# A quarter of the output projection in pieces of four matmuls between the last key tiles of attention

## The chip, the core and the metric

The kernel is one program on one core of a Trainium2 chip. The core has five engines that work side by side: TensorE (matrix products, PE in the profile, with its weight loads in a row PEld of their own), VectorE (DVE), ScalarE (ACT), GpSimd (POOL) and SyncE (SP, which here only issues DMAs). Products are accumulated in PSUM, which has eight banks of 128 x 512 numbers. The metric is the device time of one execution in microseconds; a run shown is one timed execution.

## The reference

Two blocks are applied twice to x, 2048 rows of 640 numbers, with the same weights: attention with 32 heads of 20, and a two-layer network with a squared relu. All is float32.

```python
        qkv = x @ wqkv                     # cut into q, k, v of 32 heads
        scores = jnp.einsum("bhqd,bhkd->bhqk", q, k) * (Dh ** -0.5)
        p = _softmax(scores, axis=-1)
        o = jnp.einsum("bhqk,bhkd->bhqd", p, v)
        return o.transpose(0, 2, 1, 3).reshape(B, S, D) @ wo
    x = x + _A_ref(_layernorm(x, axis=-1), A_wqkv, A_wo)
    x = x + _B_ref(_layernorm(x, axis=-1), B_w1, B_b1, B_w2, B_b2)
    # and both lines once more
```

The last product of `_A_ref`, with `wo`, is the output projection. It needs, for one row of x, the results of all 32 heads for that row.

## The kernel before

A layer is `qkv` (normalisation, projections to q, k and v, and some of the row maxima), `attention`, the output projection (`add_heads`), and `mlp`. Numbers that need full precision are kept as a high and a low half, and a product is three matmuls, high by high, high by low, low by high (`THREE`).

**Attention** works in 32 blocks (`NBLK`): 8 groups of four heads, and for each group four blocks of 512 queries (`NQB`, `QB`). A block has 16 key tiles of 128 keys (`NKT`). For one key tile TensorE forms four score tiles of 128 keys x 512 queries, one for each head (`score`, L755 of the profile). Each score matmul uses half the rows of the array, so that two run at once in two row tiles. ScalarE takes the exponential from PSUM to SBUF (`exps`, L765), and TensorE multiplies the four results with the values (`pv`, L770), eight matmuls of 32 columns each, in four column tiles. The values of all key tiles of a block gather in bank 7. Row maxima of later blocks come in between, a matmul (`smax`, L661) and a reduction on VectorE (L672).

**The order** on TensorE is a string. `ORDER_OF_BLOCK` names one letter per step: a and b are scores of one head, S is the scores of two heads with one exponential of 1024 columns, m and n are row maxima, V the values. The loop at the end of `attention` goes through the string and looks only at its end whether any row maximum is left; where none is, it goes on with `LAST_ORDER`, which has only S and V. `Clock` is a small model of the engines' times. It doesn't move any step of the string; it only says which bank a step gets, the one that it thinks free first. `clock.both` picks two neighbouring banks of 0 to 6 for an S.

**DMAs** go out on SP's queue in the order in which the program writes them; `begin` writes those that belong to a key tile as its first score is written (the dictionary `loads`, keyed by block and key tile). When a block is done, `finish` copies the sum out of bank 7, and `split` spreads the rest over the key tiles 4 to 12 of the next block: the denominators to HBM and back, their inverse on GpSimd (L814), the division (L825), the store of the block's result `ot` to `d_o`. For the very last block, inverse and division run on TensorE, VectorE and ScalarE, as `steps` that the projection takes up between its halves (`side`).

**The output projection** of a quarter of the rows (`qb`) loads five tiles `ot` of 128 of the 640 inner rows (`heads`), of which the fifth is complete only when the last group of heads is. `add_heads` then takes four tiles of 128 rows, each in two halves of 320 columns: 15 matmuls into one bank (`chain`, L336), an addition of x on VectorE (L1254), and after the second half a store to `x_mid`. Banks come from `ps_all`, a ring of all eight. After a quarter `layer` loads four slices of the weight `w_1`. Before the fourth quarter it starts `normal_rows`, which loads the first quarter's results again and normalises them for `mlp`.

Of the kernel before, what the change touches and what calls it, by code (L numbers as in the profile page):

```python
# [16 lines left out]
P = 128  # L17
# [5 lines left out]
KD = D // P  # L23
# [16 lines left out]
def tile_layers(  # L40
# [284 lines left out]
    def row_tile(src, r):  # L325
        t = xtile("x")
        dma(nc.sync, t, src[r * P : (r + 1) * P, :])
        return t
# [205 lines left out]
    class Clock:  # L534


        def __init__(self):
            self.free = [0] * 7
            self.lane, self.over, self.fresh, self.place = [0, 0], [0, 0], [False, False], 9
            self.now, self.load, self.values, self.since = 0, 0, False, 0  # L540
            self.act, self.act_end, self.dve = 0, 0, 0
            self.ready, self.used, self.acc = {}, [], 0
# [35 lines left out]
            return banks[:, b, :]  # L578

        def both(self, kt):  # L580
            b = min(range(6), key=lambda b: max(self.free[b : b + 2]))
            t = max(self.row(par, b + par) for par in range(2))
            if kt >= 3 and len(self.used) > kt - 3:
                t = max(t, self.used[kt - 3])
            t = max(t, self.act, self.act_end - 1958)
            self.act, self.act_end = t + 897, max(t + 1015, self.act_end + 910)
            self.free[b] = self.free[b + 1] = self.act_end
            self.ready[kt] = self.act_end + 80
            return banks[:, b : b + 2, :]
# [504 lines left out]
        "abmbmVbambannVbmabanmVSmbanVSnabmVSnSmVm"  # L1094
    )

    LAST_ORDER = "SSSVSSVSSVSV"

    def attention(first, x_src, first_rows):
        last = NBLK * NKT  # L1100
        es_of = {}
        e_n.clear()
        weights.extend(slot([P, 2, QB], F32, "e") for _ in range(6))
        st_n, sm_n = [0, 0], [0, 0]
        state = {"begun": -1, "done": 0, "acc": None, "debt": 0}
        clock = Clock()
        todo = [
            (t, p, sub, c)
            for t in range(NBLK)
            for c in range(4)  # L1110
            for p, sub in PAIRS
            if (t, p, sub, c) not in done
        ]
        t0 = NBLK - 4
        loads = {(t0 + 1, 2 * s): lambda s=s: w_o.load(s) for s in range(w_o.n)}
        for k in range(4):
            for qb in range(3):
                loads[t0 + 1 + qb, 2 * k + 3] = lambda qb=qb, k=k: heads(nc.sync, qb, k)
        for qb, at in ((0, (t0 + 2, 12)), (1, (t0 + 3, 1)), (2, (t0 + 3, 15))):
            loads[at] = lambda qb=qb: heads(nc.sync, qb, 4)  # L1120
        ends = {x[0]: n for n, x in enumerate(todo)}
        blocks = sorted(ends)
        firsts = {todo[0][0]: 0, **{t: ends[s] + 1 for s, t in zip(blocks, blocks[1:])}}
        over = {t for t in range(NBLK) if t not in ends and t not in done}
        rows = {"next": min(t for t in range(NBLK) if t not in done), "at": None}

        def begin(i):

            t, u = divmod(i, NKT)
            g, qb = divmod(t, NQB)  # L1130
            if u == 3:
                q_t.pop(t - 1, None)
            if u == 1:
                if t + 2 < NBLK and t + 2 not in q_t:
                    load_q(t + 2)
            if u % 4 == 1 and qb == 0:
                k_t.pop((g - 1, u // 4), None)
                for h in (0, 1, 2, 3) if g else (1, 2):
                    if g + h < NG and (g + h, u // 4) not in k_t:
                        load_k(g + h, u // 4, True)  # L1140
                if g and g + 3 >= NG:
                    del kept[(g - 1) % 4, u // 4]
            if u in (2, 10) and qb == NQB - 1 and g + 1 < NG:
                load_v(g + 1, u // 8)
            if first and t < 16 and u % 6 == 3:
                prep_job()
            if first and t < 16 and u == 8:
                for sp in (w_o, w_1, w_2):
                    sp.save_full()
                    sp.past(sp.count, sp.got)  # L1150
            if (t, u) in loads:
                loads[t, u]()
            if t == NBLK - 1 and u == 12:
                first_rows.extend(row_tile(x_src, i) for i in range(4))
            if i in split:
                split.pop(i)()

        def op(o):
            if o in "abS":
                pars = (0, 1) if o == "S" else ("ab".index(o),)  # L1160
                i, p = divmod(st_n[pars[0]], 2)
                assert len(pars) == 1 or st_n[0] == st_n[1]
                if i >= last:
                    return
                if i > state["begun"]:
                    state["begun"] = i
                    begin(i)
                es = es_of.setdefault(i, {})
                dst = clock.both(i) if o == "S" else clock.score(pars[0], i)
                for par in pars:  # L1170
                    st_n[par] += 1
                    score(
                        dst[:, par, :] if o == "S" else dst,
                        i // NKT, i % NKT, 2 * p + par, es,
                    )
                exps(es[p] if o == "S" else es[p][:, pars[0], :], dst)
            elif o in "mn":
                par = "mn".index(o)
                n = sm_n[par]
                if n == len(todo):  # L1180
                    return
                t, p, sub, c = todo[n]
                if n == firsts[t] and par == 0:
                    for s in blocks[blocks.index(t) :][:2]:
                        if s not in q_t:
                            load_q(s)
                if (t // NQB, c) not in k_t or t not in q_t:
                    return
                sm_n[par] += 1
                smax(clock.most(par), t, p, sub, c, par)  # L1190
                if n == ends[t] and min(sm_n) > n:
                    over.add(t)
                    if t * NKT > state["begun"] + 2 * NKT:
                        del q_t[t]
            else:
                i = state["done"]
                if i >= last or min(st_n) < 2 * (i + 1):
                    return
                t, u = divmod(i, NKT)
                if u == 0:  # L1200
                    state["acc"] = banks[:, 7, :]
                clock.value(i)
                pv(state["acc"], t, u, es_of.pop(i))
                state["done"] += 1
                if u == NKT - 1:
                    steps = finish(t, state["acc"])
                    split.update((i + j, f) for j, f in zip((4, 6, 7, 9, 11, 12), steps))
                t = rows["next"]
                if rows["at"] is not None:
                    if state["begun"] >= rows["at"]:  # L1210
                        mrows_load(t)
                        rows.update(next=t + 1, at=None)
                elif t in over and t in q_t and i >= (t - 2) * NKT + 2:
                    mrows_max(t)
                    mrows(t)()
                    rows["at"] = state["begun"] + 2

        for o in "abab":
            op(o)
        while state["done"] < last:  # L1220
            for o in LAST_ORDER if min(sm_n) == len(todo) else ORDER_OF_BLOCK:
                op(o)
        assert min(sm_n) == len(todo)
        q_t.clear()
        k_t.clear()
        v_t.clear()
        kept.clear()
        weights.clear()
# [4 lines left out]
    def heads(q, qb, k):  # L1233

        ot = slot([P, 2, QB], F32R, "ot")
        dma(q, ot.rearrange("p l t -> p (l t)"), d_o[k * P : (k + 1) * P, qb])
        ready.setdefault(qb, {})[k] = ot

    def add_heads(qb, x_src, x_mid, xs, side):

# [102 lines left out]
    def layer(first, x_a, x_m, x_e, front_0, ahead):  # L1343
# [5 lines left out]
                r = 32 * h + DH  # L1349
                dma(nc.sync, sums_t[r : r + 1, 32 * h : 32 * h + 32], d_one[0, :1, :32])  # L1350
        xs = []
        attention(first, x_a, xs)
        steps = []
        for i in sorted(split):
            steps += [split.pop(i), None]
# [12 lines left out]
        for qb in range(NQB):  # L1368
            if qb + 1 == NQB:
                rows = []  # L1370
                norm = normal_rows(0, x_m, rows)
                steps.extend([lambda: (next(norm, None), next(norm, None))] * 5)
            add_heads(qb, x_a, x_m, xs, side)
            for s in range(qb * 4, min(qb * 4 + 4, w_1.n)):
                w_1.load(s)
            if qb > 1:
                all_steps()
# [87 lines left out]
```

## Time and profile before

| | us |
|---|---|
| median of 3 runs | 3554.05 (3553.14 to 3554.89) |
| the profiled execution | 3553.42 |
| its span, first to last instruction | 3551.6 |
| last block of the first layer, first values to the projection's first matmul | 1345.67 to 1373.74 |
| the same in the second layer | 3112.56 to 3140.63 |

All times inside the program are microseconds from the start of the span. The granted TensorE clock is 1.00 throughout. In a row of the timeline stand start, duration, engine, line, operation, output <- inputs and number of instructions; neighbours of one kind are merged, and an idle time of the engine ahead of them stands in brackets with what ended it. The duration of a TensorE row goes to the end of its last matmul, which overlaps what follows; starts are more exact than ends. In a row of an instruction group stand count, busy time, mean duration in ns, and the idle time ahead, with who ended it.

### The profile page before, as it was taken

The page shows a single profiled execution, that of the slowest core. Times are in us where ns is not written, and L with a number is a line of the kernel's source. Part 1 is how long each engine was busy: PE and PEld are TensorE (multiplying, and loading weights), DVE is VectorE, ACT ScalarE, POOL GpSimd, SP SyncE. Part 2 cuts the span into 40 slices and gives each one's busy share as a digit, 9 for nine tenths or more (in the row PEclk, how much of TensorE's full clock was granted, in tenths as well). Part 3 has the DMA queues.
Part 4 walks back from the last instruction along what each step waited for, and adds up shares of the span by engine and source line. Part 5 has one row for each costly group of instructions (what it writes and reads, how often), then busy time and mean ns, then how long its engine had stood idle before and what let it go on. Part 6 is the DMA issues. An engine that isn't in the chain of part 4 may idle for free.

```text
span 3551.6 us, 70873 instructions
## 1 busy us (share of the span) xinstructions
PE 3541.1 (100%) x25544; PEld 2149.7 (61%) x25544; DVE 2630.1 (74%) x5090; ACT 2697.1 (76%) x4712; POOL 821.5 (23%) x935
## 2 busy tenths in 40 slices
PE   9999999999999999999999999999999999999999
PEld 8998333333333336999989973333333333379998
DVE  8998888888888881445579988888888888715443
ACT  5888999999999994122248889999999999932221
POOL 4430344321211210122153201212121211202110
PEclk9999999999999999999999999999999999999999
DMA  7766555422212236622367552222232122366221
GB/s 259 230 209 186 149 158 160 133 76 79 55 48 60 54 103 218 239 75 75 104 206 228 197 166 70 73 79 58 70 82 57 43 60 52 107 232 221 75 82 38
DMA packets 281598, 431.87 MB, mean 122 GB/s; under 512 B 70948, under 2 KB 130084, under 8 KB 281248
## 3 DMA queue, kind: packets, MB, share of 16 engines
q1 hardware_dynamic: 280720, 425.64, 38.6%
q8 instruction: 203, 3.33, 0.4%
q10 hardware_dynamic: 528, 1.70, 0.2%
q14 instruction: 147, 1.20, 0.1%
HBM read 282.52 MB, written 144.68 MB: 120 GB/s over the span
## 4 chain that ended last, share of the span: by engine, by line
PE 97%; DMA 1%; ACT 1%; DVE 0%; POOL 0%; issue 0%; SPq 0%; POOLq 0%; ACTq 0%; DVEq 0%
PE banks L770 28%; PE banks L336 22%; PE banks L755 18%; PE banks L661 17%; PE banks L356 6%; PE banks L368 5%; PE banks L351 1%; PE banks L468 0%; ACT e L765 0%; DMA x<-d_x 0%; DMA few<-d_s 0%; SPq L76 0%; DMA x<-in_A_x_dram 0%; DMA o<-d_r 0%; POOL few L814 0%
## 5 line engine op out<-in xcount | busy, mean ns | idle before, releaser
L765 ACT ACTIVATE e<-banks 128x512 f32<-128x512 f32 (+1 forms) x3416 | 2037.0, 691 | 49.7 <-PE banks L755 11.3
L672 DVE TENSOR_REDUCE mx<-banks 128x1 f32<-128x512 f32 x2560 | 1620.4, 685 | 322.5 <-PE banks L661 270.6
L770 PE MATMUL banks<-e,vg 128*32 128x512 f32 x8192 | 1093.4, 605 | 2.3 <-ACT e L765 2.1
L661 PE MATMUL banks<-k,q 60*128 60x512 f32 x3360 | 1061.8, 411 | 0.0
L755 PE MATMUL banks<-q,k 62*128 62x512 f32 x4096 | 1047.8, 441 | 0.8
L755 PEld LDWEIGHTS banks<-q,k 62*128 62x128 f32 x4096 | 515.4, 184 | 749.1 <-ACT e L765 494.2
L661 PEld LDWEIGHTS banks<-k,q 60*128 60x128 f32 x3360 | 567.9, 185 | 196.1 <-ACT e L765 65.9
L701 DVE CUSTOM_DVE_ANT_0 rl<-banks,rl 128x512 f32<-128x512 f32 x736 | 476.9, 689 | 31.1 <-PE banks L661 6.8
L694 ACT ACTIVATE rl<-banks 128x512 f32<-128x512 f32 x736 | 399.6, 602 | 56.9 <-PE banks L661 46.0
L770 PEld LDWEIGHTS banks<-e,vg 128*32 128x32 f32 x8192 | 162.2, 108 | 352.0 <-issue 269.7
L1299 ACT ACTIVATE r<-banks,b_t 128x512 f32<-128x512 f32 x96 | 66.2, 689 | 370.8 <-PE banks L336 247.2
L336 PE MATMUL banks<-w,h 128*128 128x320 f32 x2304 | 341.2, 309 | 0.0
L336 PEld LDWEIGHTS banks<-w,h 128*128 128x128 f32 x2304 | 339.1, 188 | 1.2
L336 PE MATMUL banks<-xnT,w 128*128 128x512 f32 x1440 | 329.7, 390 | 0.0
L368 PE MATMUL banks<-xnT,wqk 64*128 64x512 f32 x1080 | 326.6, 392 | 0.0
L356 PE MATMUL banks<-xnT,wqk 64*128 64x512 f32 x1080 | 325.5, 393 | 0.0
L336 PEld LDWEIGHTS banks<-xnT,w 128*128 128x128 f32 x1440 | 269.6, 188 | 55.2
L814 POOL TENSOR_TENSOR few<-few,minus_t 128x16 f32<-128x16 f32 x62 | 179.8, 2900 | 233.2 <-DMA few<-d_s 232.9
L661 PE MATMUL banks<-kd,q 60*128 60x512 f32 x736 | 211.4, 398 | 0.8 <-ACT rl L694 0.6
L356 PEld LDWEIGHTS banks<-xnT,wqk 64*128 64x128 f32 x1080 | 199.4, 187 | 12.1 <-issue 1.7
L368 PEld LDWEIGHTS banks<-xnT,wqk 64*128 64x128 f32 x1080 | 201.1, 187 | 7.7
L268 POOL CAST mr<-nt 128x32 fp32r<-128x32 f32 x64 | 13.4, 209 | 817.6 <-DVE nt L727 817.6
(94 smaller groups left out, 2709.0 us busy)
## 6 DMA issues: line engine op xcount, KB each, us to landing
q<-d_qk SPq DMA_DIRECT2D x876, 80.0 KB
d_qk<-ev SPq DMA_DIRECT2D x80, 512.0 KB
k<-d_qk SPq DMA_DIRECT2D x444, 80.0 KB
x<-d_x SPq DMA_DIRECT2D x96, 320.0 KB
d_o<-ot SPq DMA_DIRECT2D x248, 80.0 KB
ot<-d_o SPq DMA_DIRECT2D x38, 512.0 KB
d_v<-v SPq DMA_DIRECT2D x32, 512.0 KB
vg<-d_v SPq DMA_DIRECT2D x32, 512.0 KB
```

The costliest lines, as they stand in the source:

```text
L336: nc.tensor.matmul(dst, a, b, start=(n == 0), stop=(n == last))
L356: top = nc.tensor.matmul(dst, a[:64], b[:64], start=start, stop=last)
L368: low = nc.tensor.matmul(dst, a, b, start=False, stop=last, skip_group_check=True)
L661: nc.tensor.matmul(dst, q_t[t][b : b + 60, p, sub * P : (sub + 1) * P], k_t[t // NQB, c][b : b + 60, p, :], start=True, stop=True,)
L672: nc.vector.tensor_reduce(maxima(t)[:, 2 * p + par, sub, c : c + 1], dst, axis=AX.X, op=ALU.max)
L694: nc.scalar.activation(r, dst, AF.Relu)
L701: nc.vector.tensor_tensor_reduce(out=r[par], in0=dst, in1=r[par], scale=1.0, scalar=LEAST, op0=ALU.add, op1=ALU.max, accum_out=maxima(t)[: ...
L755: nc.tensor.matmul(dst, k_t[t // NQB, kt // 4][b : b + 62, p, (kt % 4) * P : (kt % 4 + 1) * P], q_t[t][b : b + 62, p, :], start=True, stop ...
L765: nc.scalar.activation(dst, src, AF.Exp, scale=SCALE)
L770: nc.tensor.matmul(acc[32 * h : 32 * h + 32, :], v_t[t // NQB, kt // 8][:, kt % 8, 32 * h : 32 * h + 32], es[p][:, par, :], start=(kt == 0 ...
L814: nc.gpsimd.tensor_tensor(few, few, minus_t, op=ALU.pow)
L1299: nc.scalar.activation(r, dst, AF.Relu, bias=b1_t[:, f : f + 1])
```

## The change

The first quarter of the output projection is taken out of `add_heads` and becomes a generator, `first_heads`. It yields after four matmuls (after three at the end of a half, behind the addition), so a half has four pieces and the quarter 32. `LAST_ORDER` gets a letter P behind each V, which takes one piece. What is left of the generator when the last values are written is run at once, ahead of the second quarter. All pieces go to bank 6, and while P is used `clock.lent` keeps `clock.both` off that bank. The fifth `ot` tile of the first quarter is loaded in key tile 13 of block 29 in place of key tile 12 of block 30, and the first four row tiles of x in key tile 15 of block 29 in place of key tile 12 of block 31. `add_heads` is called for the other three quarters.

```diff
-            self.free = [0] * 7
+            self.free, self.lent = [0] * 7, 0
...
-            b = min(range(6), key=lambda b: max(self.free[b : b + 2]))
+            b = min(range(6 - self.lent), key=lambda b: max(self.free[b : b + 2]))
...
-    LAST_ORDER = "SSSVSSVSSVSV"
-
-    def attention(first, x_src, first_rows):
+    LAST_ORDER = "SSSVPSSVPSSVPSVP"
+
+    def attention(first, load_rows, out):
...
-        for qb, at in ((0, (t0 + 2, 12)), (1, (t0 + 3, 1)), (2, (t0 + 3, 15))):
+        loads[t0 + 1, 15] = load_rows
+        for qb, at in ((0, (t0 + 1, 13)), (1, (t0 + 3, 1)), (2, (t0 + 3, 15))):
...
-            if t == NBLK - 1 and u == 12:
-                first_rows.extend(row_tile(x_src, i) for i in range(4))
...
+            elif o == "P":
+                next(out, None)
...
-            for o in LAST_ORDER if min(sm_n) == len(todo) else ORDER_OF_BLOCK:
+            clock.lent = int(min(sm_n) == len(todo))
+            for o in LAST_ORDER if clock.lent else ORDER_OF_BLOCK:
                 op(o)
+        for _ in out:
+            pass
...
+    def first_heads(x_src, x_mid, xs):
+
+        ot, dst = ready.pop(0), banks[:, 6, :]
+        for i in range(4):
+            xs.append(row_tile(x_src, 4 + i))
+            x = xs.pop(0)
+            for hf in range(2):
+                pairs = [
+                    (ot[k][:, hx, i * P : (i + 1) * P], w_o.piece(k * 4 + hw * 2 + hf))
+                    for k in range(KD)
+                    for hx, hw in THREE
+                ]
+                for n, (a, b) in enumerate(pairs):
+                    nc.tensor.matmul(
+                        dst[:, :HALF], a, b, start=(n == 0), stop=(n + 1 == len(pairs))
+                    )
+                    if n % 4 == 3:
+                        yield
+                c = slice(hf * HALF, (hf + 1) * HALF)
+                nc.vector.tensor_add(x[:, c], dst[:, :HALF], x[:, c])
+                if hf:
+                    dma(nc.sync, x_mid[i * P : (i + 1) * P, :], x)
+                yield
...
-            add_heads(qb, x_a, x_m, xs, side)
+            if qb:
+                add_heads(qb, x_a, x_m, xs, side)
```

How this stands on TensorE in the first layer, at the beginning of the last block (L755 scores, L770 values, q_14464 the last block's queries; the second layer is the same). Before:

```order
L755 MATMUL banks<-q_14464,k_4826 128x512 x6
L770 MATMUL banks<-e_5384,vg_14330 32x512 x2
L770 MATMUL banks<-e_5383,vg_14330 32x512 x2
L755 MATMUL banks<-q_14464,k_4826 128x512 x4
L770 MATMUL banks<-e_5386,vg_14330 32x512 x2
L770 MATMUL banks<-e_5385,vg_14330 32x512 x2
L755 MATMUL banks<-q_14464,k_4826 128x512 x2
```

And now, L1256 being the new projection's matmul:

```order
L755 MATMUL banks<-q_14464,k_4826 128x512 x6
L770 MATMUL banks<-e_5384,vg_14330 32x512 x2
L770 MATMUL banks<-e_5383,vg_14330 32x512 x2
L1256 MATMUL banks<-wo_14894,ot_14973 128x320 x3
L1256 MATMUL banks<-wo_14943,ot_15013 128x320
L755 MATMUL banks<-q_14464,k_4826 128x512 x4
L770 MATMUL banks<-e_5386,vg_14330 32x512 x2
L770 MATMUL banks<-e_5385,vg_14330 32x512 x2
L1256 MATMUL banks<-wo_14992,ot_15013 128x320
L1256 MATMUL banks<-wo_14943,ot_15013 128x320
L1256 MATMUL banks<-wo_14992,ot_15050 128x320
L1256 MATMUL banks<-wo_15032,ot_15050 128x320
```

The first P stands behind the first key tile of the last block, since the string ahead of `LAST_ORDER` runs to its end; with 16 key tiles left, 16 of the 32 pieces find a place there.

On TensorE right behind the last values, with what each row waits for: before, the first half followed by the second, in the next bank of the ring,

```order
L336 MATMUL banks<-wo_15106,ot_15447 128x320
L336 MATMUL banks<-wo_15152,ot_15447 128x320
L336 MATMUL banks<-wo_15106,ot_15447 128x320
L336 MATMUL banks<-wo_14894,ot_14973 128x320 x3
L336 MATMUL banks<-wo_14943,ot_15013 128x320
```

and now the end of the fourth half, the start of the fifth, which waits for VectorE,

```order
L1256 MATMUL banks<-wo_15106,ot_15172 128x320
L1256 MATMUL banks<-wo_15152,ot_15172 128x320
L1256 MATMUL banks<-wo_15106,ot_15172 128x320
L1256 MATMUL banks<-wo_14894,ot_14973 128x320 [waits DVE_49]
L1256 MATMUL banks<-wo_14894,ot_14973 128x320 x2
L1256 MATMUL banks<-wo_14943,ot_15013 128x320
```

and the end of the eighth half with the first of the second quarter, which in this layer gets bank 6 from the ring:

```order
L1256 MATMUL banks<-wo_15106,ot_15172 128x320
L1256 MATMUL banks<-wo_15152,ot_15172 128x320
L1256 MATMUL banks<-wo_15106,ot_15172 128x320
L336 MATMUL banks<-wo_14894,ot_15289 128x320 [waits DVE_49]
L336 MATMUL banks<-wo_14894,ot_15289 128x320 x2
```

Five such waits stand there in the first layer and four in the second, where the ring is at bank 3 by then.

On SP's queue in block 29, before and now (`wo` and `ot` are loads of the projection, `d_o` is the store of block 28, `d_s` the denominators of block 29):

```order
L76 DMA d_o<-ot_15108 20x1024 x4
L76 DMA wo_15152<-d_wo 128x640
L76 DMA d_s<-o_15234 1x512 x4
L76 DMA ot_15279<-d_o 128x1024
L76 DMA few_15236<-d_s 128x16
```

```order
L76 DMA d_o<-ot_15108 20x1024 x4
L76 DMA wo_15152<-d_wo 128x640
L76 DMA ot_15172<-d_o 128x1024
L76 DMA x_15207<-in_A_x_dram 128x640
L76 DMA x_15209<-in_A_x_dram 128x640
L76 DMA x_15211<-in_A_x_dram 128x640
L76 DMA x_15213<-in_A_x_dram 128x640
L76 DMA d_s<-o_15244 1x512 x4
L76 DMA ot_15289<-d_o 128x1024
L76 DMA few_15246<-d_s 128x16
```

The load of the fifth `ot` tile and the four rows of x now stand ahead of block 29's denominators.

More of the change, by code (lines that the diff above doesn't have):

```diff
@@ L1351, in layer, with load_rows @@
         xs = []
-        attention(first, x_a, xs)
+        def load_rows():
+            xs.extend(row_tile(x_a, i) for i in range(4))
+        attention(first, load_rows, first_heads(x_a, x_m, xs))
         steps = []
```

## The prediction

> **What bounds the kernel now.** I read the page first (busy times and the chain that ended last), then the same views cut to the stretch that the change touches.
>
> ```profile
> span 3551.6 us, 70873 instructions
> ...
> PE 3541.1 (100%) x25544; PEld 2149.7 (61%) x25544; DVE 2630.1 (74%) x5090; ACT 2697.1 (76%) x4712; POOL 821.5 (23%) x935
> ```
>
> TensorE's row reads 100%, which would leave no room for anything. That row is modelled, so I looked at who waits in the attention's tail, after the last row maximum. The first row below is the table of stretches (length, then busy time of PE, PEld, DVE, ACT, POOL, then clock and DMA); the others are instruction groups of the same stretch.
>
> ```profile
> 1345.67:1367.67 22.00, 21.72 (x146) 6.13 (x144) 0.00 (x0) 22.00 (x25) 6.07 (x4) 1.00 0.45 137
> ```
>
> ```profile
> L765 ACT ACTIVATE e<-banks 128x1024 f32<-128x1024 f32 x25 | 23.1, 1123 | 0.0
> ...
> L755 PEld LDWEIGHTS banks<-q,k 62*128 62x128 f32 x48 | 4.2, 183 | 13.0 <-ACT e L765 10.5 <-issue 2.5
> ```
>
> ScalarE is busy for 22.00 of 22.00 us, and the score weights idle 10.5 us until one of its exponentials ends. So ScalarE bounds the tail, at 22.00 / 12 key tiles = 1.83 us each. The idle is not all free. In the tail's rows in order of time
>
> ```profile
> 1346.67 0.19 PEld L755 LDWEIGHTS banks<-q,k 62*128 62x128 f32 x2 [0.84 <-ACT e L765]
> ...
> 1347.08 0.19 PEld L755 LDWEIGHTS banks<-q,k 62*128 62x128 f32 x2 [0.23 <-ACT e L765]
> ```
>
> the first idle, 0.84 us, is the running time of the values ahead; only a part of the second is a wait. What is free must come from TensorE's pace where nothing holds it:
>
> ```profile
> 1331.04 0.73 PE L755 MATMUL banks<-q,k 62*128 62x512 f32 x4
> 1331.70 1.07 PE L770 MATMUL banks<-e,vg 128*32 128x512 f32 x8
> 1332.69 0.74 PE L755 MATMUL banks<-q,k 62*128 62x512 f32 x4
> ...
> 1345.67 1.06 PE L770 MATMUL banks<-e,vg 128*32 128x512 f32 x8
> ...
> 1350.34 0.49 PE L755 MATMUL banks<-q,k 62*128 62x512 f32 x2
> 1350.76 1.06 PE L770 MATMUL banks<-e,vg 128*32 128x512 f32 x8
> ...
> 1372.75 1.06 PE L770 MATMUL banks<-e,vg 128*32 128x512 f32 x8 [0.76 <-ACT e L765]
> 1373.74 2.46 PE L336 MATMUL banks<-wo,ot 128*128 128x320 f32 x15
> ```
>
> Start to start, one key tile's values take 0.99 us (1331.70 to 1332.69), two pairs of scores 0.66 (1331.04 to 1331.70), one pair 0.42 to 0.43 (1350.34 to 1350.76). So a group of scores is 0.20 plus 0.23 a pair. In the sixteen key tiles from 1345.67 to the projection's start at 1373.74 there are 27 pairs in 14 groups: TensorE needs 16 x 0.99 + 27 x 0.23 + 14 x 0.20 = 24.9 us and is given 28.1. **Its real slack is 3.2 us.** In the second layer the same stretch is as long, 3140.63 - 3112.56 = 28.07:
>
> ```profile
> 3112.56 1.07 PE L770 MATMUL banks<-e,vg 128*32 128x512 f32 x8
> ...
> 3140.63 2.46 PE L336 MATMUL banks<-wo,ot 128*128 128x320 f32 x15
> ```
>
> Behind it the projection is TensorE's alone; the chain in order of time has
>
> ```profile
> 1373.81 2.39 PE banks L336 x15
> 1376.20 0.86 PE banks L796 x2
> 1377.06 50.61 PE banks L336 x345
> ```
>
> which is 50.61 / 345 = 0.1467 us a matmul, with no wait between the halves of 15.
>
> **The change, part by part.** Pieces come out of the generator once per P, and P exists only in LAST_ORDER. The order of the program shows that the pattern ahead of it runs to its end first, so that P begins behind the first key tile of the last block: 16 of the 32 pieces (60 matmuls, four halves) lie behind values, the last of them behind the very last values. The other 16 (60 matmuls) run straight after attention, all into bank 6.
>
> *Removed.* Per layer 60 matmuls leave the stretch behind attention, less the last piece's 3, which still follow the last values: 57 x 0.1467 = 8.4 us.
>
> *Added inside attention.* 57 matmuls, 8.4 us, in 15 pieces, and for each piece a further change of the array's shape, from four column tiles to the whole array to two row tiles. The trace has no such piece. Nearest are transposes (whole array) followed by 64-row tiles:
>
> ```profile
> 38.42 1.29 PEld L468 LDWEIGHTS banks<-ident,x 128*128 128x128 f32 x12 [0.35 <-issue]
> ...
> 39.88 0.18 PEld L356 LDWEIGHTS banks<-xnT,wqk 64*128 64x128 f32 x1 [0.17 <-issue]
> ...
> 40.78 0.86 PEld L468 LDWEIGHTS banks<-ident,x 128*128 128x128 f32 x8 [0.36 <-issue]
> ...
> 41.80 0.18 PEld L356 LDWEIGHTS banks<-xnT,wqk 64*128 64x128 f32 x1 [0.16 <-issue]
> ```
>
> Twelve take 1.46 us and eight 1.02, so 0.11 each and 0.14 on top; a group of scores has 0.20 on top. A matmul of 320 columns lies between 128 and 512, so I take 0.20, with ends 0 (the weights come in unseen, as within a projection) and 0.25: 15 x 0.20 = 3.0 us. TensorE then needs 24.9 + 8.4 + 3.0 = 36.3 us where it had 28.1: **attention grows by 8.2 us**, and TensorE is the bound there in ScalarE's place. What was gained behind is given back in front: 8.2 - 8.4 = -0.2 us a layer.
> The Trainium skill (TensorEngine Tiling (Array Packing), Tiling Modes, Key Properties) says that a change of tiling mode drains TensorE. By that rule every piece pays, as I charged; without it the 3.0 us go, and the two layers come out 6 us lower. The rows above bear the rule out for transposes; no row shows a piece.
>
> *Added behind attention.* Each of the remaining halves starts in the bank that the half before it leaves to VectorE's add, and now waits for it. Before, halves went round eight banks. The price is a sum of rows:
>
> ```profile
> 1376.30 0.49 DVE L1254 TENSOR_TENSOR x<-banks,x 128x320 f32<-128x320 f32 x1 [1.64 <-PE banks L336]
> ```
>
> ```profile
> 1445.18 0.53 DVE x L252
> 1445.71 0.04 issue
> 1445.75 2.07 PE banks L1276 x17
> ```
>
> From the half's first weights (1373.74) to the add's start (1376.30) 2.56 us, the add 0.49, VectorE to TensorE 0.04: 3.09 us a half where 15 x 0.1467 = 2.20 was enough, so 0.89 a wait. The fifth to eighth half pay it, four a layer. In the first layer the ring of banks gives the next half bank 6 too (its first matmul waits for VectorE in the order), in the second bank 3: nine waits, 9 x 0.89 = **8.0 us**. Its ends are 0.6 (the next weights come in during the add) and 1.0. While TensorE waits there, only these adds run on VectorE.
>
> *Nothing, with its cover.* VectorE's adds inside attention: its busy time there is 0.00 us above, and a bank is asked for again only a key tile later. The lent bank: the pairs of banks used by the exponentials are three of the six that remain, as before. SP gets five DMAs earlier, in block 29 (ot of the last heads, four rows of x); they stand ahead of that block's sums:
>
> ```profile
> 1306.93 1.41 SPq L76 DMA_DIRECT2D d_o<-ot  x4
> 1308.44 0.35 SPq L76 DMA_DIRECT2D wo<-d_wo  x1
> 1313.44 1.10 SPq L76 DMA_DIRECT2D d_s<-o  x4
> ...
> 1367.78 1.81 SPq L76 DMA_DIRECT2D x<-in_A_x_dram  x4
> ```
>
> There SP has 4.6 us free, and five issues take some 2.3. If the ot load waits there for the stores ahead of it, the sums are late by a few us, and the next to be late is that block's division on GpSimd, which idles 9.19 us before it:
>
> ```profile
> 1330.76 0.21 POOL L268 CAST mr<-nt 128x32 fp32r<-128x32 f32 x1 [9.19 <-DVE nt L727]
> ```
>
> SP's later stores of finished rows wait for VectorE's adds with the fourth quarter's four ot loads and w1's first four behind them, until some 12 us after attention; those ot are used 36 us later, and the longest landing on the chain is this one:
>
> ```profile
> 1430.57 7.32 DMA x<-d_x
> ```
>
> The last block's inversion and division move from the first quarter's halves to the second's, and have 34 us instead of 52 to the fourth quarter, for 7 halves and two transfers.
>
> **The sum.** 2 x (8.2 - 8.4) + 8.0 = +7.6 us. The profiled execution took 3553.42 us (1.8 around its span); it becomes 3561.0. The median of the runs, 3554.05, lies 0.6 above it: 3561.7, so I say 3562.
>
> **The rivals.**
> - *Faster: ScalarE stays the bound.* If the pieces fit into the 10.5 us of idle, attention doesn't grow: -2 x 8.4 + 8.0 = -8.8, 3545. It decides where four key tiles with 15 matmuls need at most ScalarE's 7.33 us; by the rows they need 4 x 0.99 + 8 x 0.23 + 4 x 0.20 + 2.2 + 4 x 0.20 = 9.6. For it speaks only the idle itself. The Trainium skill (Perfetto Trace Analysis, Optimization Strategy) says that interleaving stretches with different busiest engines may help, which is this rival; the trace gives the slack for 3.2 us a layer of it.
> - *Unchanged: a piece costs only its matmuls.* Without the 0.20, 30 x 0.20 = 6.0 us less: 3556. For it, weights are loaded behind running matmuls inside a projection; against it, the 0.16 and 0.17 us of idle at the changes above.
> - *Slower still: the pieces starve ScalarE as well.* Scores start 0.8 us later in each key tile. If the group with one pair then leaves the next values waiting for an exponential, one of 0.92 (22.00 / 24) in each of 3.75 rounds a layer, it costs 7 us more: 3569. Against it, exponentials run two or three ahead.
>
> **How the numbers follow.** A measurement of this kernel tells 0.2%, 7.1 us, from no change: "within" ends at 3561.2, next to my sum. Forecast 0.58, own range 3559 to 3565 (wait 0.8 to 1.0, piece 0.16 to 0.25), of which 0.38 lies beyond 3561.2, since what I haven't seen is likelier a wait than a gain; unchanged 0.15; slower still 0.20; faster 0.07. Slower 0.58, within 0.35, faster 0.07. The range takes in the second and third rival and leaves out the first: 3555 to 3569.
>
> **What would show it.** Right: values 2.4 us apart from the last block's first key tile on, ScalarE with idle before each exponential, weight loads no longer waiting for it; the projection's first matmul outside attention 8 us later; four gaps of 0.9 us a layer, with VectorE's add as releaser, and a fifth in the first. Wrong: values still 1.83 us apart (first rival); pieces with no idle around them (second); values that wait for exponentials, or a wait on a load behind SP (third).

## The result: 3560.03 us, 6.1 us over the time before

| | before | after |
|---|---|---|
| median of 18 runs each, us | 3553.95 (3552.99 to 3555.91) | 3560.03 (3559.23 to 3562.50) |
| ratio of the times, 95% interval | | 1.0018 (1.0011 to 1.0024) |
| the profiled execution, us | 3553.42 | 3559.76 |
| its span, us | 3551.6 | 3558.0 |

The interval, times 3554 us, is +3.9 to +8.5 us. The time lies 2 us under the predicted 3562, inside the range, and within 0.2% of the time before, though only by 1 us.

The page's row of busy times is almost what it was, and tells nothing of the change:

```profile
PE 3544.4 (100%) x25544; PEld 2145.3 (60%) x25544; DVE 2628.9 (74%) x5090; ACT 2699.9 (76%) x4712; POOL 821.5 (23%) x935
```

The table of stretches, cut to the same place as before and then to the whole last block of the first layer, and two instruction groups of that block (columns as in the prediction):

```profile
1345.63:1367.63 22.00, 22.00 (x148) 9.43 (x150) 0.98 (x2) 17.92 (x20) 6.08 (x4) 1.00 0.50 152
1345.63:1381.83 36.20, 36.20 (x242) 15.22 (x240) 1.47 (x3) 28.20 (x30) 6.08 (x4) 1.00 0.42 132
```

```profile
L765 ACT ACTIVATE e<-banks 128x1024 f32<-128x1024 f32 x30 | 28.9, 1037 | 6.4 <-PE banks L755 6.3
...
L755 PEld LDWEIGHTS banks<-q,k 62*128 62x128 f32 x54 | 4.3, 184 | 2.8 <-issue 2.1 <-ACT e L765 0.6
```

ScalarE, which had been busy for 22.00 of 22.00 us, is now busy for 17.92, and over the whole block its exponentials wait 6.3 us for scores from TensorE. The score weights, which had waited 10.5 us for ScalarE in 22 us, wait 0.6 in 36. The bound has passed from ScalarE to TensorE. TensorE's timeline shows the new round: values (L770), a piece (L1256), scores (L755), then the last values and what stands behind them.

```profile
1345.63 1.07 PE L770 MATMUL banks<-e,vg 128*32 128x512 f32 x8
1346.63 0.85 PE L1256 MATMUL banks<-wo,ot 128*128 128x320 f32 x4
1347.41 0.73 PE L755 MATMUL banks<-q,k 62*128 62x512 f32 x4
1348.07 1.07 PE L770 MATMUL banks<-e,vg 128*32 128x512 f32 x8
...
1353.70 0.70 PE L1256 MATMUL banks<-wo,ot 128*128 128x320 f32 x3
1354.34 0.96 PE L755 MATMUL banks<-q,k 62*128 62x512 f32 x6
...
1381.83 0.71 PE L1256 MATMUL banks<-wo,ot 128*128 128x320 f32 x3
1383.19 2.46 PE L1256 MATMUL banks<-wo,ot 128*128 128x320 f32 x15 [0.65 <-DVE x L1262]
1386.23 2.46 PE L1256 MATMUL banks<-wo,ot 128*128 128x320 f32 x15 [0.58 <-DVE x L1262]
...
1395.37 2.47 PE L336 MATMUL banks<-wo,ot 128*128 128x320 f32 x15 [0.58 <-DVE x L1262]
```

A piece of four takes 1347.41 - 1346.63 = 0.78 us, a piece of three 0.64. The first two key tiles' values are 2.44 us apart; four key tiles take 1355.23 - 1345.63 = 9.60 us, 2.40 each, which is what the prediction had added up for four with 15 matmuls. From the block's first values to the end of its last the stretch is now 1381.83 - 1345.63 = 36.20 us, where it was 28.07: **attention grew by 8.13 us**. In the second layer it is 3152.88 - 3116.69 = 36.19:

```profile
3116.69 1.06 PE L770 MATMUL banks<-e,vg 128*32 128x512 f32 x8
...
3152.88 0.71 PE L1256 MATMUL banks<-wo,ot 128*128 128x320 f32 x3
...
3165.69 2.37 PE L336 MATMUL banks<-wo,ot 128*128 128x320 f32 x15
```

Behind attention each half in bank 6 starts 1386.23 - 1383.19 = 3.04 to 3.05 us behind the one before, where 2.20 were enough: **a wait costs 0.85 us** (the first a little more, 0.92). The first layer has five of them, the second four (its next half, at 3165.69, starts with no wait). The chain in order of time gives the parts of one:

```profile
1383.19 2.48 PE banks L1256 x15
...
1385.69 0.50 DVE x L1262
...
1386.23 2.47 PE banks L1256 x15
```

One difference isn't in the prediction at all. At the end of the projection TensorE transposes the first quarter's normalised rows. Before, it began and then waited for VectorE (L252 writes the normalised rows). The rows are first those of before, in both layers, then those of after.

```profile
1445.10 0.49 PE L1276 MATMUL banks<-ident,x 128*128 128x128 f32 x3
1445.75 2.07 PE L1276 MATMUL banks<-ident,x 128*128 128x128 f32 x17 [0.17 <-DVE x L252]
1447.58 1.64 PE L336 MATMUL banks<-xnT,w 128*128 128x512 f32 x6
...
3211.99 0.82 PE L1276 MATMUL banks<-ident,x 128*128 128x128 f32 x3
3213.41 2.08 PE L1276 MATMUL banks<-ident,x 128*128 128x128 f32 x17 [0.59 <-DVE x L252]
3215.24 2.09 PE L336 MATMUL banks<-xnT,w 128*128 128x512 f32 x8
```

```profile
1449.14 2.34 PE L1304 MATMUL banks<-ident,x 128*128 128x128 f32 x20
1451.24 2.10 PE L336 MATMUL banks<-xnT,w 128*128 128x512 f32 x8
...
3219.36 2.47 PE L1304 MATMUL banks<-ident,x 128*128 128x128 f32 x20
3221.58 1.63 PE L336 MATMUL banks<-xnT,w 128*128 128x512 f32 x6
```

From the first transpose to the product behind it were 2.48 and 3.25 us, and are 2.10 and 2.22: 0.38 and 1.03 us less. With this the two profiled executions can be reckoned up. First layer: 8.13 - 57 x 0.1467 + 5 x 0.85 - 0.38 = +3.64, and the row behind the transposes stands 1451.24 - 1447.58 = 3.66 later. Second layer: 8.12 - 8.36 + 4 x 0.85 - 1.03 = +2.13. Between the layers 0.47 more are lost (the second layer's last block begins 4.13 later, not 3.66). One wait of that size stands there in this execution and not in that of before: 0.46 us for a DMA, ahead of a matmul of row maxima (L661) at 1808.80. Whether it makes the loss isn't shown, because the matmuls around it follow each other in another order. Together +6.2; the spans differ by 6.4.

### The profile page after: what moved, and what is told of

The parts are those of the page before. It is cut to its first block, busy times and chain, and to the rows that moved or that the text cites. A ratio compares the mean times of both kernels' runs of the same rounds, so it can differ in the third digit from the quotient of the medians.

```text
span 3558.0 us, 70857 instructions
## 1 busy us (share of the span) xinstructions
PE 3544.4 (100%) x25544; PEld 2145.3 (60%) x25544; DVE 2628.9 (74%) x5090; ACT 2699.9 (76%) x4712; POOL 821.5 (23%) x935
## 4 chain that ended last, share of the span: by engine, by line
PE 98%; ACT 1%; DVE 0%; issue 0%; DMA 0%; POOL 0%; DVEq 0%; ACTq 0%
PE banks L770 28%; PE banks L336 22%; PE banks L755 18%; PE banks L661 17%; PE banks L356 5%; PE banks L368 5%; PE banks L1256 1%; PE banks L351 1%; PE banks L468 0%; ACT e L765 0%; DVE x L1262 0%; PE banks L1304 0%; ACT rl L694 0%; DVE bst L244 0%; DMA d_qk<-ev 0%
## 5 line engine op out<-in xcount | busy, mean ns | idle before, releaser
L770 PE MATMUL banks<-e,vg 128*32 128x512 f32 x8192 | 1093.5, 605 | 0.7 <-ACT e L765 0.7
L661 PE MATMUL banks<-k,q 60*128 60x512 f32 x3360 | 1060.2, 410 | 0.5 <-DMA d_qk<-ev 0.5
L755 PE MATMUL banks<-q,k 62*128 62x512 f32 x4096 | 1043.6, 440 | 0.2
L755 PEld LDWEIGHTS banks<-q,k 62*128 62x128 f32 x4096 | 514.2, 184 | 723.5 <-ACT e L765 469.9
L661 PEld LDWEIGHTS banks<-k,q 60*128 60x128 f32 x3360 | 567.7, 185 | 198.5 <-ACT e L765 65.8
L770 PEld LDWEIGHTS banks<-e,vg 128*32 128x32 f32 x8192 | 162.1, 108 | 352.4 <-issue 274.4
L661 PE MATMUL banks<-kd,q 60*128 60x512 f32 x736 | 211.2, 398 | 0.8 <-ACT rl L694 0.6
L268 POOL CAST mr<-nt 128x32 fp32r<-128x32 f32 x64 | 13.4, 210 | 823.5 <-DVE nt L727 823.5
```

Source lines behind the costliest of these rows:

```text
L661: nc.tensor.matmul(dst, q_t[t][b : b + 60, p, sub * P : (sub + 1) * P], k_t[t // NQB, c][b : b + 60, p, :], start=True, stop=True,)
L755: nc.tensor.matmul(dst, k_t[t // NQB, kt // 4][b : b + 62, p, (kt % 4) * P : (kt % 4 + 1) * P], q_t[t][b : b + 62, p, :], start=True, stop ...
L770: nc.tensor.matmul(acc[32 * h : 32 * h + 32, :], v_t[t // NQB, kt // 8][:, kt % 8, 32 * h : 32 * h + 32], es[p][:, par, :], start=(kt == 0 ...
```

## The experiments

Edits are shown against the changed kernel. Each table of results gives the median of the runs, its ratio to the kernel before in the same comparison, and the ratio's 95% interval. Kernels before measured 3553.41 us in the first four experiments' comparison, 3553.16 in the last three's.

### Is it the bank, the pieces, or the moved loads?

**The drained pieces in two banks.** Bank 6 is used as long as attention lasts. Behind it, halves alternate between banks 1 and 2, so that the next half needn't wait for VectorE's addition.

```diff
-        ot, dst = ready.pop(0), banks[:, 6, :]
+        ot = ready.pop(0)
...
+                dst = banks[:, 6 if i < 2 else 1 + hf, :]
```

> The four halves that run behind attention alternate between banks 1 and 2 in place of bank 6; the pieces inside attention stay. Theory (the loss is the nine waits for VectorE's add, 0.85 us each in the trace of the changed kernel, and the pieces inside attention give back what they take): 9 x 0.85 = 7.6 us less than the changed kernel, about 3552.4, level with the kernel before or a little under it. Rival (the pieces inside attention are the loss, and the waits only hide something that would be waited for anyway): 3560, as the changed kernel.

**No pieces inside attention.** The order of before, so that all eight halves stand behind attention, in the one bank.

```diff
-    LAST_ORDER = "SSSVPSSVPSSVPSVP"
+    LAST_ORDER = "SSSVSSVSSVSV"
```

> No P in the order: nothing of the projection inside attention, all eight halves behind it, all in bank 6; the loads stay where the change put them. Theory (waits): attention takes 28.1 us again from its last block's first values to its end, the eight halves pay seven waits in each layer and the first layer's next half an eighth, so 15 x 0.85 = 12.7 us over the kernel before: 3566 to 3567, and 5 to 6 us over the changed kernel. Rival (the pieces are the loss): near the kernel before, 3554.

**No pieces, two banks.** Both edits, with all eight halves in banks 1 and 2. What is left of the change is the order of the DMAs, the place of the last block's inversion and division, and the lent bank.

```diff
-    LAST_ORDER = "SSSVPSSVPSSVPSVP"
+    LAST_ORDER = "SSSVSSVSSVSV"
...
-        ot, dst = ready.pop(0), banks[:, 6, :]
+        ot = ready.pop(0)
...
+                dst = banks[:, 1 + hf, :]
```

> Neither pieces nor one bank: all eight halves behind attention, alternating between banks 1 and 2. What is left of the change are the earlier loads and the order on SP. Theory: 3554, as the kernel before, within 1 us. Rival (the moved loads and SP's order cost or gain something themselves): off by more than 2 us either way.

| | us | ratio |
|---|---|---|
| the change | 3560.03 | 1.0018 (1.0011 to 1.0024) |
| pieces, two banks behind | 3551.85 (3551.11 to 3556.07, 11 runs) | 0.9996 (0.9987 to 1.0004) |
| no pieces, one bank | 3565.80 (3565.31 to 3566.67, 5 runs) | 1.0032 (1.0020 to 1.0045) |
| no pieces, two banks | 3553.20 (3552.36 to 3557.02, 11 runs) | 0.9999 (0.9990 to 1.0008) |

All three came out within a microsecond of their theories, and 8 us or more from the two rivals that named a time. With two banks the waits are gone. Timeline of that kernel (the projection's matmul is L1257 there):

```profile
1345.61 1.06 PE L770 MATMUL banks<-e,vg 128*32 128x512 f32 x8
...
1381.90 9.50 PE L1257 MATMUL banks<-wo,ot 128*128 128x320 f32 x63
1391.24 2.36 PE L336 MATMUL banks<-wo,ot 128*128 128x320 f32 x15
```

63 matmuls in 1391.24 - 1381.90 = 9.34 us are 0.148 each, while attention is as long as in the changed kernel, 1381.90 - 1345.61 = 36.29 us. The ratio falls by 0.0022, or 7.8 us (the two intervals reach 0.0007 and 0.0009 to either side); nine waits of 0.85 are 7.7. Without the pieces but with one bank there are fifteen (eight in the first layer, seven in the second). The first half and the first wait on the timeline:

```profile
1374.65 2.47 PE L1256 MATMUL banks<-wo,ot 128*128 128x320 f32 x15
1377.76 2.48 PE L1256 MATMUL banks<-wo,ot 128*128 128x320 f32 x15 [0.64 <-DVE x L1262]
```

That kernel and the one with two banks and no pieces differ by 12.6 us in one comparison, 12.6 / 15 = 0.84 a wait. So two differences of kernels, by other edits and other counts, give the price that the timeline gives. It follows that the slowdown is the one bank. The pieces as placed are worth little: by the timeline they give 0.2 us a layer, by the medians 1.4 us in all (3551.85 against 3553.20), and the two intervals overlap. That the moved loads, the moved division and the lent bank cost nothing is shown to some 3 us, the half width of the third interval, and no better.

The third kernel also settles the transposes. It has no piece, its transposes begin 1.0 us later than before in both layers, as all of its projection does, and still:

```profile
1446.11 2.45 PE L1305 MATMUL banks<-ident,x 128*128 128x128 f32 x20
...
3213.04 2.36 PE L1305 MATMUL banks<-ident,x 128*128 128x128 f32 x20
```

Neither layer's transposes wait. So it doesn't take the pieces to lose that wait; and two kernels below that have pieces show it again, 0.59 us in the second layer. Upstream of it stand the loads of the finished rows: in the first layer, from their issue to the first statistics on VectorE, 7.3 us in the profile of before, 7.0 in that of the change, 7.1 here, and 6.6 to 6.9 in the others. In the second layer, where most of the wait was, it is 7.7 before, 6.9 in the change and here, and 7.6 and 7.3 in the two that wait again, where VectorE then waits 0.96 and 0.55 us more for another of these loads. Two that don't wait have 7.3 and 7.4 without that. So the loads are the likely cause, and not a shown one. This execution loses about as much at another load, that of row maxima for the last block:

```profile
1344.10 0.47 PE L755 MATMUL banks<-q,k 62*128 62x512 f32 x1 [0.80 <-DMA q<-d_m]
```

Of all the profiles only this one has that wait. A single profile can't tell whether the moved loads make it likelier.

### What does a change of shape cost, and can it be saved?

**Pieces of eight and seven.** A half goes in two pieces instead of four, behind every second key tile. As many matmuls lie inside attention, with half the changes of shape.

```diff
-    LAST_ORDER = "SSSVPSSVPSSVPSVP"
+    LAST_ORDER = "SSSVSSVPSSVSVP"
...
-                    if n % 4 == 3:
+                    if n == 7:
```

> Pieces of eight and seven matmuls behind every second key tile's values, in place of four behind each; one bank as in the change. It halves the changes of the array's shape (7 pieces between values and scores in place of 15). If each piece's 0.2 us is all that stands beside its matmuls, attention is 8 x 0.2 = 1.6 us shorter in each layer, and 4 matmuls less lie inside: 3556.8. Rival (a longer piece lets ScalarE run dry, whose wait takes the place of what is saved): attention as long as in the changed kernel, 3560 to 3561, with idle ahead of ScalarE's exponentials and values that wait for them.

It took 3561.09 us (3560.32 to 3563.28, 11 runs), ratio 1.0020 (1.0011 to 1.0029): nothing saved. Its timeline for one round of four key tiles:

```profile
1349.26 1.43 PE L1256 MATMUL banks<-wo,ot 128*128 128x320 f32 x8
1350.63 0.73 PE L755 MATMUL banks<-q,k 62*128 62x512 f32 x4
...
1356.82 0.50 PE L755 MATMUL banks<-q,k 62*128 62x512 f32 x2
1357.53 0.51 PE L755 MATMUL banks<-q,k 62*128 62x512 f32 x2 [0.21 <-ACT e L765]
1357.96 1.06 PE L770 MATMUL banks<-e,vg 128*32 128x512 f32 x8
```

A piece of eight takes 1350.63 - 1349.26 = 1.37 us = 8 x 0.1467 + 0.20, so **a piece costs 0.20 us beside its matmuls whatever its length**, and this kernel does save that for every second piece. But three times a block two pairs of scores take 1357.96 - 1356.82 = 1.14 us in place of the 0.66 that two pairs take elsewhere, since the second pair waits for ScalarE to free its banks. The 0.48 us of this eat the two changes saved (0.40). The last piece, behind the last values, is also longer by four matmuls. The block's last values come 1382.40 - 1346.35 = 36.05 us behind the first, ahead of that last piece, where the changed kernel took 36.20. So the rival was right about the price. About the sign it was not: what waits in each round are scores, and values wait for an exponential only at the block's end (0.19 us). That ScalarE is late there because its scores came late, behind the longer piece, is how I read it; the bracket shows only that TensorE waits for it.

### Where should a piece stand?

**Whole halves behind the first of every four key tiles,** with two banks. As few changes of shape as there can be for four halves.

```diff
-    LAST_ORDER = "SSSVPSSVPSSVPSVP"
+    LAST_ORDER = "SSSVPSSVSSVSV"
...
-                    if n % 4 == 3:
-                        yield
```

(and the two banks as in the first experiment)

> Whole halves of 15 matmuls as pieces, one in each round of four key tiles, behind the values that follow three pairs of scores (where ScalarE has most work queued); behind attention two banks in turn. Four changes of the array's shape between values and scores in place of 15. Theory (a step model of the two engines from the measured durations: ScalarE works on through the piece from its queue): attention grows by 7.2 us for 8.8 us of matmuls moved, 1.3 us a layer better than with pieces of four, so 3549.3. Rival A (only the changes of shape count, 0.2 us each): 6.4 us for 8.8, 3547.4. Rival B (2.2 us without scores starve ScalarE, as with the eights): no better than the run with two banks, 3552 or more.

**The same behind the third of every four.**

```diff
-    LAST_ORDER = "SSSVPSSVPSSVPSVP"
+    LAST_ORDER = "SSSVSSVSSVPSV"
```

> The same four whole halves with the same number of changes of shape, but behind the third key tile of each round, ahead of the one pair of scores that the next values need. Theory (what is queued on ScalarE at that place decides): attention grows by 8.5 us for 8.8, as much as with pieces of four: 3551.8, 2.5 us over the run with the halves in the first place. Rival A (only the number of matmuls and of changes counts): both places equal.

**The same as the first of these, but begun earlier:** the string ahead of `LAST_ORDER` is left as soon as the row maxima are done, so that six halves find a place inside attention.

```diff
             for o in LAST_ORDER if clock.lent else ORDER_OF_BLOCK:
                 op(o)
+                if not clock.lent and o == "V" and min(sm_n) == len(todo) and st_n[0] == st_n[1]:
+                    break
```

(and `6 if i < 3`)

> As the run with the halves in the first place, and the last order starts as soon as the last row maximum is written, some eight key tiles sooner, in place of at the end of the long string; six halves then lie inside attention and two behind it. Theory: in each layer some 1.0 us less, since eight key tiles go at 1.83 us in place of 1.95 (exponentials of 1024 columns only), and two more halves gain 0.4 us each: 3546 to 3547. Rival (the slack of these key tiles is already used, or the row maxima's load for the last block, which arrives just in time, now stops TensorE): 3549 to 3551, with a wait on that load.

| | us, 11 runs each | ratio |
|---|---|---|
| halves behind the first of four | 3548.84 (3548.29 to 3551.47) | 0.9988 (0.9979 to 0.9997) |
| halves behind the third of four | 3551.96 (3550.81 to 3557.20) | 0.9998 (0.9989 to 1.0007) |
| six halves, from earlier on | 3549.57 (3548.86 to 3553.14) | 0.9991 (0.9982 to 1.0000) |

The first beats both kernels: 4.3 us under the time before (1.1 to 7.5 by the interval; all its 11 runs lie under the lowest of the 27 before), 11 under the change, which was measured in another comparison. The same round of four key tiles, on the timeline of the first and then of the second:

```profile
1346.63 2.46 PE L1257 MATMUL banks<-wo,ot 128*128 128x320 f32 x15
1349.02 0.73 PE L755 MATMUL banks<-q,k 62*128 62x512 f32 x4
...
1355.79 2.46 PE L1257 MATMUL banks<-wo,ot 128*128 128x320 f32 x15
...
1381.03 9.06 PE L1257 MATMUL banks<-wo,ot 128*128 128x320 f32 x60
```

```profile
1350.38 2.46 PE L1257 MATMUL banks<-wo,ot 128*128 128x320 f32 x15
1352.77 0.50 PE L755 MATMUL banks<-q,k 62*128 62x512 f32 x2
...
1356.09 0.50 PE L755 MATMUL banks<-q,k 62*128 62x512 f32 x2
1356.79 0.49 PE L755 MATMUL banks<-q,k 62*128 62x512 f32 x2 [0.21 <-ACT e L765]
1357.21 1.07 PE L770 MATMUL banks<-e,vg 128*32 128x512 f32 x8
...
1360.05 2.46 PE L1257 MATMUL banks<-wo,ot 128*128 128x320 f32 x15
```

A round takes 1355.79 - 1346.63 = 9.16 us in the first and 1360.05 - 1350.38 = 9.67 in the second, with the same matmuls. Most of the difference of 0.51 is again two pairs of scores that take 1.12 instead of 0.66. Behind the first key tile two pairs of scores follow the half; behind the third only one does. That ScalarE so gets too little work after its wait is my reading; that the place alone makes the wait is shown. Over the block this is 1.25 us a layer (1381.03 - 1345.63 = 35.40 against 36.65), 2.5 in all, of the 3.1 that the medians show (ten of the first kernel's 11 runs lie under the lowest of the second's). Against the 28.07 of before, attention grew by 7.33 and 8.58 us a layer, where 7.2 and 8.5 were expected. So both theories held, the rival in which the place makes no difference fell, and for the first kernel 2 x (8.80 - 7.33) = 2.9 of the 4.3 us are accounted for.

The third kernel missed its theory, 3546 to 3547, by some 3 us. The two early halves cost as much inside attention as they save behind it:

```profile
1330.05 1.06 PE L770 MATMUL banks<-e,vg 128*32 128x512 f32 x8
1331.04 1.20 PE L755 MATMUL banks<-q,k 62*128 62x512 f32 x5
1332.68 0.50 PE L755 MATMUL banks<-q,k 62*128 62x512 f32 x1 [0.44 <-ACT e L765]
1333.12 1.07 PE L770 MATMUL banks<-e,vg 128*32 128x512 f32 x8
1334.11 2.46 PE L1259 MATMUL banks<-wo,ot 128*128 128x320 f32 x15
...
1349.96 1.06 PE L770 MATMUL banks<-e,vg 128*32 128x512 f32 x8 [0.48 <-DVE o L783]
```

The eight key tiles from 1330.05 to the last block's first values take 1349.96 - 1330.05 = 19.91 us, and took 1345.67 - 1330.04 = 15.6 before: 4.3 more, against 30 x 0.1467 = 4.4 saved. There was slack there: with 17 pairs in eight groups TensorE's need, by the prediction's own figures, is 8 x 0.99 + 17 x 0.23 + 8 x 0.20 = 13.4 of 15.6, so 2.2 us, about what my theory had put in (2.3). What it had left out is what used it up. The two pieces cost 0.4 beside their matmuls. The first three pairs of scores take 1333.12 - 1331.04 = 2.08 us in place of 0.89; the bracket shows the last score waiting for ScalarE. And the last block's first values wait 0.48 for the copy of the block before out of bank 7. Together these are 2.1 us. The second layer shows the same two waits and the same 19.91 us. So the rival had the size right and the reason wrong: the slack was not used already, and the wait on the load of row maxima that it named isn't on TensorE's timeline.

## Why the prediction was right, and where it leaned wrong

**Who bounds, and the real slack of 3.2 us: right.** The growth was 8.13 and 8.12 us a layer for a predicted 8.2. ScalarE's 10.5 us of apparent room were worth three, as TensorE's pace without waits had said. This is what refutes the rival that was faster: the values are 2.40 us apart on average and not 1.83.

**The change of shape, 0.20: right,** though taken from score groups and transposes. Pieces of four, eight and fifteen cost 0.19, 0.20 and 0.19 (2.39 - 2.20) beside their matmuls. So the rival in which a piece costs only its matmuls falls in each trace. The rule of the Trainium skill (TensorEngine Tiling (Array Packing), Key Properties) that a switch drains TensorE agrees with these rows. They don't show it alone: a matmul more costs (2.39 - 0.78) / 11 = 0.146 within a piece and 0.1467 over the halves one behind the other, so a new half costs nothing by itself and the 0.20 belongs to the borders between a piece and other work; that it is the change of shape there is inferred.

**Nine waits of 0.89: right in number and place, 0.04 too long each,** 0.4 us in all. The mis-sized part is the way from a half's first matmul to the addition's start, taken as 2.56 us from the first half of the projection, and 2.50 here. "Only these adds run on VectorE" was wrong for the first wait: its addition stands behind the copy out of bank 7 (L783), its idle time is 0.65 rather than 0.58, and the wait 0.92.

**The pieces starve ScalarE as well, 3569: not in the change,** where ScalarE's idle comes from TensorE and no values wait for an exponential in any round. But something near it exists: with pieces of eight and seven, or a half ahead of a single pair, it is the next scores that wait for ScalarE, and this costs 0.5 us a round.

**What was costed at nothing** (SP's queue, the lent bank, the moved division) showed no cost that the runs can tell from nothing. The traces say a little more. The sums of block 29 were late, as feared (their inverse on GpSimd begins at 1321.14, and began at 1318.67), but the division behind them was not (1331.24 against 1331.26). And without pieces, attention takes 28.19 to 28.37 us in the two kernels that have none, where it took 28.07; the lent bank may be the reason, which no run separates.

**The chances leaned to the wrong side of a line.** The sum was +7.6, half a microsecond above the 7.1 that a measurement can tell, and the step that put the larger chance on slower was that what wasn't seen is "likelier a wait than a gain". The terms as measured give 2 x (8.12 - 8.36) + 9 x 0.85 = +7.2. What wasn't seen was a gain, 1.4 us at the transposes, less the 0.47 between the layers. Since a kernel with no pieces has that gain too, it seems to belong to how long loads take in one execution or another; this is not shown. So on which side of the line the time fell was decided by something that no step of the sum had in it. A sum made against a single profiled execution carries such an error of about 1 us, and a sum 0.5 from a line can't say on which side the time falls.

## What to carry to other kernels

Slack is what the engine that gets the new work has left, counted from its own pace where nothing holds it; the idle time of its rows promised three times as much here. Since a change of shape costs the same for four matmuls as for fifteen, pieces put between other work should be few and long, but they then must stand where enough work for the next engine follows them. And an accumulator that goes to a reader between two uses needs a second bank: the one bank cost 7.7 us here, more than the best of these kernels gained (4.3).

## What the runs showed that was not expected

- The place of a piece, with the same matmuls and as many pieces, was worth 3.1 us by the medians (3548.84 against 3551.96) and 2.5 by the timelines. I had taken the slack to be one sum over the block; it is also a matter of each round.
- One late group of scores costs more than its wait: a bracket of 0.21 us on the timeline went with 0.46 to 0.48 us more from start to start. The two pairs then no longer follow each other as one group: two single pairs take 2 x 0.43 = 0.86 and the wait 0.21, together 1.07 of the 1.12 to 1.14 seen, where a group of two takes 0.66.
- Loads of the same rows at the same place took 6.6 to 7.7 us, from their issue to the first use, over these kernels' profiles, and a wait of some 0.4 to 1.0 us behind them came and went with no edit that I could find to account for it.
